# Attention decode with a fixed order of key and value tiles: two value tiles in one run of TensorE's loop, and whole landings for all keys but the last tile

## The chip, the cores and the metric

The kernel runs on one core of one Trainium2 chip. The metric is device time in microseconds (us) of one execution; a profile of one execution shows where it goes. "Span" is the time from the first to the last instruction of the program in that profile.

## The reference

One query per head attends to 65,536 keys. There are 32 query heads and 8 key/value heads (G = 8 in the kernel), so four query heads share one key/value head. All inputs and the output are bf16.

```python
B, Hq, Hkv, Sq, Sk, D = 1, 32, 8, 1, 65536, 128
scores = jnp.einsum("bhqd,bhkd->bhqk", q, k) * D ** -0.5
p = softmax(scores, axis=-1)
out = jnp.einsum("bhqk,bhkd->bhqd", p, v)
```

Keys and values together are 8 heads x 2 x 65,536 x 128 x 2 bytes = 268.4 MB, each byte read once.

## The kernel before, in words

**Tiles.** The keys of a head, and its values, are each cut into two tiles. A tile is 128 partitions x 256 rows (NT) x 128 elements, 64 KB in a partition and 8.4 MB in all. I write k0,1 for the second key tile of head 0 and v6,0 for the first value tile of head 6. There are 32 tiles and a ring of three buffers in SBUF (`buf`), so a tile can be asked for only when the tile three places earlier has been used up.

**Order of the tiles** (list `tiles`, L153 to L156): k0,0 k0,1 k1,0 k1,1 v0,0; then for each head g from 2 to 7 the four tiles kg,0 kg,1 v(g-2),1 v(g-1),0; then v6,1 v7,0 v7,1. All loads are issued by SyncE (SP) through `load` (L132), in that order, on one DMA queue. Before the load number `at`, SP waits for the use of tile `at - 3` (L161 to L169):

```python
if was == "k":
    sp.wait_ge(*((kb, wh + 1) if ws else (clr, 4 * wh + 3)))
else:
    if (wh, ws) not in BY:
        sp.wait_ge((sC, sD)[ws], 16 * (wh + 1)).then_inc(sV, NT // STEP)
    sp.wait_ge(vit, NT // STEP * (2 * wh + ws + 1))
```

`clr` is raised when TensorE clears one of its four score banks of a head; the third clear of a head (`4 * wh + 3`) tells that the head's first key tile has been read. `kb` is raised by VectorE once all four banks of the head are summed. `vit` is raised after each 32 value rows. A tile is loaded by one DMA or by several to consecutive rows; each DMA raises a semaphore of its own, so the first rows can be used before the last have landed. Before the change k0,0, k0,1, k7,0 and k7,1 come in two halves each, v6,0 and v6,1 in 128 + 128 rows, v7,0 in 128 + 64 + 64 (`BY`, L22 to L24), v7,1 in eight pieces (`PIECES`, L28).

**VectorE (DVE)** transposes each half of a key tile in place (`turn`, L312, the transpose at L318), waiting for that half's semaphore `sK[b][x]` (L315). Where a key tile lands by one DMA, the second half's semaphore has been raised beforehand by ScalarE (L254 to L258). After the four halves of a head comes the block `turned` (L365): it waits for the four score banks, copies a small value (L327, which raises `kb`), transposes half of the weights of the head before (L323), takes the maximum (L370), and exchanges a few small results with TensorE until the reciprocal at L337. Then it loops to the next head's keys.

**TensorE (PE)** runs a loop written out by blocks with its counters in registers. `turn` waits for the head's query weights (`wqs`); `bank` waits for one transposed half (`kt`), clears a score bank (L451, a matmul at L418) and runs 32 matmuls on it (L460), four banks a head. Then, from head 2 on, `values` (L479) runs v(g-2),1: each round takes one unit of `sV` and runs 8 matmuls on 32 value rows (L484). `summed` closes the sum of a head (L501), finds the common maximum (L504) and starts the next sum (L509, L511). Then `values` runs v(g-1),0 and control returns to `turn`. Register `x` tells `values_done` whether to go to `turn` (5) or on to `summed`; register `e` tells where a run of value rows ends. After the last keys `turn` goes to the block `late` (L518), which sets `e`, and from there to `values`. `tail` (L524) takes the last 64 rows of v7,1 as their pieces land.

**GpSimd (POOL)** passes the landings of the pieced value tiles on to `sV` (L215 to L220); after v6,0 it also waits for `outs` to reach 8 and raises `wqs` by 2, for the two late passes through `turn`. **ScalarE (ACT)** loads the queries (L227), takes the exponentials (L244) and writes the outputs.

Of the kernel before, what the change touches and what calls it, by code (L numbers as in the profile page):

```python
# [9 lines left out]
ALU = mybir.AluOpType  # L10
# [3 lines left out]
G = 8  # L14
# [3 lines left out]
NT = 256  # L18
# [1 line left out]
C = 16  # L20
SLIDE = P + 4 * (W - 1)
BY = {  # L22
    (G - 2, 0): (128, 128), (G - 2, 1): (128, 128), (G - 1, 0): (128, 64, 64),
}  # L24
N = 2
FAR = 2.0 ** 126
# [1 line left out]
PIECES = (64, 64, 32, 32, 44, 8, 8, 4)  # L28
MOVED = 4
# [3 lines left out]
def kernel(  # L33
# [18 lines left out]
    _, Hkv, Sk, _ = k.shape  # L52
# [5 lines left out]
    pe, dve, act, pool, sp = nc.tensor, nc.vector, nc.scalar, nc.gpsimd, nc.sync  # L58
# [37 lines left out]
    def sem(name):  # L96
        sems.append(nc.alloc_semaphore(name))
        return sems[-1]

    sK = [[sem(f"sK{b}{x}") for x in range(2)] for b in range(3)]  # L100
# [11 lines left out]
    wqs = sem("wqs")  # L112
# [7 lines left out]
    outs = sem("outs")  # L120
# [4 lines left out]
    cleared = list(sems)  # L125
# [3 lines left out]
    kr = [k[0, g].rearrange("(p n) d -> p (n d)", p=P) for g in range(G)]  # L129
    vr = [v[0, g].rearrange("(p n) d -> p (n d)", p=P) for g in range(G)]  # L130

    def load(at, src, s, lo=0, n=NT):  # L132
        at = at % 3 * half + lo * D
        return sp.dma_start(  # L134
            out=buf[:, at:at + n * D], in_=src[:, s * half + lo * D:s * half + (lo + n) * D]
        )

    first = load(0, kr[0], 0, 0, NT // 2)  # L140
    tc.no_tile_sem_insts.add(first.ins.name)
    first.then_inc(sK[0][0], 16)
    tc.add_to_no_dep_group("first", first.ins)
# [3 lines left out]
    tc.compile()  # L147


    load(0, kr[0], 0, NT // 2, NT // 2).then_inc(sK[0][1], 16)  # L150
    load(1, kr[0], 1, 0, NT // 2).then_inc(sK[1][0], 16)
    load(1, kr[0], 1, NT // 2, NT // 2).then_inc(sK[1][1], 16)
    tiles = [("k", 0, 0), ("k", 0, 1), ("k", 1, 0), ("k", 1, 1), ("v", 0, 0)]  # L153
    for g in range(2, G):
        tiles += [("k", g, 0), ("k", g, 1), ("v", g - 2, 1), ("v", g - 1, 0)]
# [2 lines left out]
    for at, (kind, h, s) in enumerate(tiles):  # L158
        if at < 2:
            continue  # L160
        if at > 2:  # L161
            was, wh, ws = tiles[at - 3]
# [4 lines that stand above are left out]
                if (wh, ws) not in BY:  # L167
                    sp.wait_ge((sC, sD)[ws], 16 * (wh + 1)).then_inc(sV, NT // STEP)
                sp.wait_ge(vit, NT // STEP * (2 * wh + ws + 1))  # L169
        if kind == "k" and h == G - 1:  # L170
            for x in range(2):
                load(at, kr[h], s, x * NT // 2, NT // 2).then_inc(sK[at % 3][x], 16)
        elif kind == "k":
            load(at, kr[h], s).then_inc(sK[at % 3][0], 16)
        elif (h, s) == (G - 1, 1):
            lo = 0
            for n, land in zip(PIECES, sP):
                load(at, vr[h], s, lo, n).then_inc(land, 16)
                lo += n
        elif (h, s) in BY:  # L180
            lo = 0
            for n in BY[h, s]:
                load(at, vr[h], s, lo, n).then_inc(lands.pop(0), 16)
                lo += n
        else:
            load(at, vr[h], s).then_inc((sC, sD)[s], 16)
# [29 lines left out]
    for at, (land, n) in enumerate(list(zip(sL, sum(BY.values(), ()))) + list(zip(sP, PIECES))[:MOVED]):  # L216

        pool.wait_ge(land, 32 if land is sP[0] else 16).then_inc(sV, n // STEP)
        if at + 1 == len(BY[G - 2, 0]):
            pool.wait_ge(outs, G).then_inc(wqs, 2)  # L220

    def take(engine, semaphore, n=1):

        engine.wait_ge(semaphore, n).then_inc(semaphore, -n)  # L224


    act.dma_start(out=qn, in_=q[0, :, 0, :]).then_inc(sQ, 16)  # L227
    act.wait_ge(qps, 1)
    act.copy(
        out=qx[:, :].rearrange("p (b r h) -> p b h r", b=2, r=2),  # L230
# [10 lines left out]
    for g in range(G + 1):  # L241
        if g < G:
            act.wait_ge(nms, g + 1)
            act.activation(  # L244
                out=E[:, :], in_=sc[:, :], func=ACT.Exp, bias=nmb[:, 0:1], scale=SCALE,
                accum_out=o_r[:, D:D + 1],
            ).then_inc(exd, 1)

        act.wait_ge(rls, g + 1)
        at = max(g - 1, 0) * D  # L250
        act.activation(  # L251
            out=o_out[:, at:at + D], in_=psum_f[0:H, 0:D], func=ACT.Copy, scale=rl
        ).then_inc(outs, 1)
        if g == 0:  # L254

            for b in range(3):
                n = sum(kind == "k" and at % 3 == b and 0 < h < G - 1 for at, (kind, h, _) in enumerate(tiles))
                act.nop().then_inc(sK[b][1], 16 * n)  # L258
    act.wait_ge(outs, G + 1)
    store(1, 0, G - 1)  # L260
    act.wait_ge(end, 1)
# [7 lines left out]
    def value(reg, below):  # L269
        return bass.RuntimeValue.of_register_unchecked(reg, min_val=0, max_val=below - 1)  # L270
# [68 lines left out]
    def block_of(engine):  # L339

        return lambda name: nc.body(name, parent=home, valid_engines=[engine.engine])

    block = block_of(dve)
    r_h, r_k = dve.alloc_register("h"), dve.alloc_register("k")
    h, kb_at = value(r_h, G + 1), value(r_k, 3)
# [61 lines left out]
    def counter(name, below):  # L407

        reg = pe.alloc_register(name)
        return reg, value(reg, below)  # L410

    block = block_of(pe)

    def add(reg, n, op=ALU.add):
        pe.reg_alu(reg, reg, n, op)

    def clear(bank, lhsT=zer[:, 0:P], rhs=zer):
        return pe.matmul(out=bank, lhsT=lhsT, rhs=rhs, start=True, stop=False)  # L418

    def close(bank):  # L420
        return pe.matmul(  # L421
            out=bank[:, 0:1], lhsT=zer[:, 0:P], rhs=zer[:, 0:1], start=False, stop=True
        )
# [5 lines left out]
    def chosen(out, start, n=D):  # L429

        return pe.matmul(out=out[0:H, 0:n], lhsT=sel[:, :], rhs=o_r[:, 0:n], start=start, stop=True)  # L431

    r_g, g = counter("g", G + 2)
    r_x, x = counter("x", 6)
    r_p, p = counter("p", ring)
    r_s, s = counter("s", 4 * W)
    r_w, w = counter("w", 2049)
    r_e, e = counter("e", 2049)
# [15 lines left out]
    with block("scores"):  # L454
        bank = sc[:, ds(value(r_x, 4) * 512, 512)]
        slide = value(r_s, 4 * (W - N) + 1)
        keys = value(r_p, ring - half // 2 + (W - N) * D + 1)
        for y in range(4 * N):
            m, n = y % 4, y // 4
# [40 lines left out]
    with block("summed"):  # L500
        close(psum_o[:, :]).then_inc(vdone, 1)  # L501
        take(pe, mxs)

        pe.matmul(  # L504
            out=misc[:, :], lhsT=same[:, :], rhs=each[:, :].unsqueeze(1).broadcast_to([P, 16, 32]),
            start=True, stop=True,
        ).then_inc(pes, 1)
        take(pe, mxs)
        clear(psum_o[:, :], away, rows4[:, :])  # L509
        pe.reg_mov(r_x, 5)  # L510
        chosen(psum_f, True, D + 1).then_inc(pes, 1)  # L511
        add(r_g, 1)
        pe.br_ne(g, 1, on_true="values", on_false="turn")
    with block("turn"):
        take(pe, wqs)
        pe.reg_mov(r_x, 0)
        pe.br_lt(g, G, on_true="bank", on_false="late")
    with block("late"):  # L518

        pe.reg_alu(r_e, r_g, 4 * (sum(PIECES[:MOVED]) - NT), ALU.mult)  # L520
        add(r_e, 2048 - 4 * G * (sum(PIECES[:MOVED]) - NT))
        pe.br("values")

    with block("tail"):  # L524
        at = sum(PIECES[:MOVED])
# [62 lines left out]
```

## Time and profile before

| What | us |
|---|---|
| Median of three runs (lowest, highest) | 628.53 (628.41, 628.55) |
| The profiled execution's own time | 628.39 |
| Its span | 626.5 |
| Time outside the span | 1.9 |
| PE busy / DVE busy within the span | 504.5 / 331.4 |

A row of a timeline has the start in us from the span's beginning, the length in us, the engine, the line, the operation, what is written and read, how many instructions were merged, and in brackets the idle time of the engine just before and what ended it. "PEq" and "DVEq" are the sequencers of the engines: their waits on semaphores end the idle time, whoever raised the semaphore. SPq rows are DMA issues, and all of them stand under L134. In a view by stages, PEclk is the TensorE clock that was granted, as a share of full speed.

### The profile page before, as it was taken

Reading aid. Unit: us, or ns where it says so; the run is one execution under the profiler, and the core shown is the slowest. Engines: PE = TensorE matmul, PEld = TensorE weight load, DVE = VectorE, ACT = ScalarE, POOL = GpSimd, SP = SyncE. Lnnn points to the kernel's source line nnn. Section 1 sums busy time; section 2 is a strip of 40 time slices with the busy share of each in tenths; the row PEclk is TensorE's granted clock in tenths of the full one; section 3 lists DMA queues with packets and bytes.
Section 4 is the critical chain, followed back from the end, with each engine's and each line's share of the span. In section 5 each row is a group of like instructions: output and inputs, shape, how many; then the busy total and the mean of one; then the engine's idle time right before and its main releaser. Section 6 shows DMA issues by size and latency. Waiting matters only on the chain. (4 is left out here: it accounts for less than half of the span.)

```text
span 626.5 us, 8015 instructions
## 1 busy us (share of the span) xinstructions
PE 504.5 (81%) x2186; PEld 204.2 (33%) x2186; DVE 331.4 (53%) x109; ACT 21.1 (3%) x28; POOL 6.0 (1%) x16
## 2 busy tenths in 40 slices
PE   0587299798994889948799397993979988799997
PEld 0232043243331333313333133331433333333333
DVE  3983895789214892148821588215872389410100
ACT  1000100100010000100001000010000100001000
POOL 2000000000000000000000000000000000000000
PEclk9998589799998789988899889997899998999999
DMA  9999999999999999999999999999999999999997
GB/s 371 433 469 402 469 402 469 402 460 410 452 418 423 448 402 469 402 469 402 469 402 469 402 469 402 469 402 469 402 464 406 418 425 429 435 435 435 423 431 319
DMA packets 6857, 268.46 MB, mean 429 GB/s; under 512 B 840, under 2 KB 968, under 8 KB 1224
## 3 DMA queue, kind: packets, MB, share of 16 engines
q1 hardware_dynamic: 6768, 268.44, 99.4%
q10 hardware_dynamic: 88, 0.02, 0.0%
q14 instruction: 1, 0.01, 0.0%
HBM read 268.44 MB, written 0.01 MB: 429 GB/s over the span
## 5 line engine op out<-in xcount | busy, mean ns | idle before, releaser
L318 DVE STREAM_TRANSPOSE buf<-buf 128x8192 f32<-128x8192 f32 x32 | 277.2, 8694 | 87.2 <-DVEq L224 87.2
L460 PE MATMUL sc<-buf,zeros 128*128 x1024 | 247.8, 401 | 0.0
L484 PE MATMUL psum_o<-buf,Ew 128*16 x1008 | 226.0, 382 | 11.7 <-PEq L224 11.0
L460 PEld LDWEIGHTS sc<-buf,zeros 128*128 x1024 | 102.3, 100 | 137.7 <-issue 41.6
L484 PEld LDWEIGHTS psum_o<-buf,Ew 128*16 x1008 | 89.3, 89 | 145.2 <-issue 54.9
L418 PE MATMUL sc<-zeros 128*128 128x512 bf16 x32 | 13.8, 432 | 87.8 <-PEq L224 87.8
L331 DVE TENSOR_REDUCE o_r<-psum_o 128x128 f32<-128x512 f32 x10 | 6.9, 688 | 100.2 <-DVEq L224 72.4
L327 DVE COPY o_r<-o_r 4x1 f32<-4x1 f32 x9 | 1.3, 142 | 79.7 <-DVEq L224 65.6
L418 PEld LDWEIGHTS sc<-zeros 128*128 128x128 bf16 x32 | 3.1, 98 | 97.1 <-issue 96.0
L244 ACT ACTIVATE zeros<-sc,nmb 128x2048 bf16<-128x2048 f32 x8 | 15.7, 1967 | 535.9 <-DVE nmb L382 535.9
L323 DVE STREAM_TRANSPOSE Ew<-zeros 128x1024 bf16<-128x1024 bf16 x18 | 22.3, 1240 | 14.0 <-PE psum_o L484 14.0
L504 PE MATMUL misc<-each,same 128*128 128x512 f32 x18 | 11.3, 712 | 8.6 <-PEq L224 8.6
L370 DVE TENSOR_REDUCE mx<-sc 128x1 f32<-128x2048 f32 x8 | 18.0, 2253 | 0.0
L441 PE MATMUL misc<-Ew 32*128 32x128 bf16 x1 | 0.3, 283 | 10.7 <-DVE Ew L308 10.7
L208 POOL TENSOR_TENSOR zeros<-qx,quad 128x64 bf16<-128x64 bf16 x8 | 2.4, 294 | 486.6 <-ACT o_out L251 480.4
L504 PEld LDWEIGHTS misc<-each,same 128*128 128x128 f32 x18 | 2.9, 202 | 8.9 <-issue 8.8
L421 PE MATMUL sc<-zeros 128*128 128x1 bf16 x32 | 5.2, 163 | 0.0
L418 PE MATMUL psum_o<-rows,zeros 4*128 4x512 bf16 x10 | 4.5, 451 | 0.0
L289 DVE CAST Ew<-ident 32x128 bf16<-32x128 f32 x1 | 3.0, 2984 | 2.7 <-POOL ident L193 2.7
L421 PEld LDWEIGHTS sc<-zeros 128*128 128x128 bf16 x32 | 3.0, 95 | 3.9
L251 ACT ACTIVATE o_out<-psum_f,o_r 4x128 bf16<-4x128 f32 x9 | 3.1, 345 | 29.3 <-DVE o_r L337 29.3
L431 PE MATMUL psum_f<-o_r,sel 128*4 128x129 f32 x18 | 3.9, 302 | 0.0
(32 smaller groups left out, 31.9 us busy)
## 6 DMA issues: line engine op xcount, KB each, us to landing
buf<-in_k_dram SPq DMA_DIRECT2D x8, 4096.0 KB, 28.5
buf<-in_v_dram SPq DMA_DIRECT2D x5, 4096.0 KB, 32.5
buf<-in_v_dram SPq DMA_DIRECT2D x4, 2048.0 KB, 36.4
buf<-in_v_dram SPq DMA_DIRECT2D x2, 1024.0 KB, 38.7
buf<-in_v_dram SPq DMA_DIRECT2D x1, 1408.0 KB, 42.6
buf<-in_v_dram SPq DMA_DIRECT2D x2, 256.0 KB, 40.6
buf<-in_k_dram SPq DMA_DIRECT2D x12, 34.6
buf<-in_v_dram SPq DMA_DIRECT2D x12, 34.4
```

What stands on the lines that cost most here:

```text
L244: act.activation(out=E[:, :], in_=sc[:, :], func=ACT.Exp, bias=nmb[:, 0:1], scale=SCALE, accum_out=o_r[:, D:D + 1],).then_inc(exd, 1)
L251: act.activation(out=o_out[:, at:at + D], in_=psum_f[0:H, 0:D], func=ACT.Copy, scale=rl).then_inc(outs, 1)
L318: dve.transpose(out=kv, in_=kv).then_inc(kt, 1)
L323: return dve.transpose(out=Ew[:, at], in_=E[:, at])
L331: return dve.tensor_reduce(out=o_r[:, 0:D], in_=psum_o[:, :].rearrange("p (y d) -> p d y", y=4), axis=AX.X, op=ALU.max)
L370: after(dve.tensor_reduce(out=mx[:, :], in_=sc[:, :], axis=AX.X, op=ALU.max))
L418: return pe.matmul(out=bank, lhsT=lhsT, rhs=rhs, start=True, stop=False)
L421: return pe.matmul(out=bank[:, 0:1], lhsT=zer[:, 0:P], rhs=zer[:, 0:1], start=False, stop=True)
L431: return pe.matmul(out=out[0:H, 0:n], lhsT=sel[:, :], rhs=o_r[:, 0:n], start=start, stop=True)
L460: pe.matmul(out=bank, lhsT=moved(wq[:, m * SLIDE + 4 * n:][:, 0:P], slide), rhs=moved(T[:, n, m // 2, m % 2], keys), start=False, stop=False,)
L484: last = pe.matmul(out=psum_o[0:16, :], lhsT=moved(Ew[:, column(4 * j + 3):][:, 0:16], weight), rhs=moved(buf[:, 4 * j * D:][:, 0:4 * D], ...
L504: pe.matmul(out=misc[:, :], lhsT=same[:, :], rhs=each[:, :].unsqueeze(1).broadcast_to([P, 16, 32]), start=True, stop=True,).then_inc(pes, 1)
```

## The change

1. k0,0, k0,1 and k7,0 land by one DMA each; only k7,1 is still cut in halves. ScalarE's raising of the second halves' semaphores covers them now, and stands ahead of its first wait instead of after head 0.
2. v6,0 lands by one DMA, v7,0 by two of 128 rows instead of three. v6,1 (two) and v7,1 (eight) are as they were.
3. TensorE sets `e` for the late runs in `summed`, between its first and second exchange with VectorE, and leaves `x` as it is there. So v6,0 and v6,1 are one run of `values`, and so are v7,0 and the first 192 rows of v7,1; neither passes through `values_done` and `turn` in its middle. The `wqs` signal for these passes is gone; GpSimd still holds v6,1 back until `outs` is 8. Heads below 8 pass through a new small block `first`, which sets `x` to 5 as `summed` did.

```diff
 BY = {
-    (G - 2, 0): (128, 128), (G - 2, 1): (128, 128), (G - 1, 0): (128, 64, 64),
+    (G - 2, 0): (NT,), (G - 2, 1): (128, 128), (G - 1, 0): (128, 128),
 }
...
-    first = load(0, kr[0], 0, 0, NT // 2)
+    first = load(0, kr[0], 0)
...
-    load(0, kr[0], 0, NT // 2, NT // 2).then_inc(sK[0][1], 16)
-    load(1, kr[0], 1, 0, NT // 2).then_inc(sK[1][0], 16)
-    load(1, kr[0], 1, NT // 2, NT // 2).then_inc(sK[1][1], 16)
+    load(1, kr[0], 1).then_inc(sK[1][0], 16)
...
-        if kind == "k" and h == G - 1:
+        if (kind, h, s) == ("k", G - 1, 1):
...
         if at + 1 == len(BY[G - 2, 0]):
-            pool.wait_ge(outs, G).then_inc(wqs, 2)
+            pool.wait_ge(outs, G)
...
     act.dma_start(out=qn, in_=q[0, :, 0, :]).then_inc(sQ, 16)
+
+    for b in range(3):
+        n = sum(kind == "k" and at % 3 == b and (h, s) != (G - 1, 1) for at, (kind, h, s) in enumerate(tiles))
+        act.nop().then_inc(sK[b][1], 16 * n)
     act.wait_ge(qps, 1)
...
-        if g == 0:
-
-            for b in range(3):
-                n = sum(kind == "k" and at % 3 == b and 0 < h < G - 1 for at, (kind, h, _) in enumerate(tiles))
-                act.nop().then_inc(sK[b][1], 16 * n)
...
         ).then_inc(pes, 1)
+        add(r_g, 1)
+        pe.br_lt(g, G, on_true="first", on_false="late")
+    with block("late"):
+
+        pe.reg_alu(r_e, r_g, 4 * (sum(PIECES[:MOVED]) - NT), ALU.mult)
+        add(r_e, 2048 - 4 * G * (sum(PIECES[:MOVED]) - NT))
+        pe.br("cleared")
+    with block("first"):
+        pe.reg_mov(r_x, 5)
+        pe.br("cleared")
+    with block("cleared"):
         take(pe, mxs)
         clear(psum_o[:, :], away, rows4[:, :])
-        pe.reg_mov(r_x, 5)
         chosen(psum_f, True, D + 1).then_inc(pes, 1)
-        add(r_g, 1)
         pe.br_ne(g, 1, on_true="values", on_false="turn")
     with block("turn"):
         take(pe, wqs)
         pe.reg_mov(r_x, 0)
-        pe.br_lt(g, G, on_true="bank", on_false="late")
-    with block("late"):
-
-        pe.reg_alu(r_e, r_g, 4 * (sum(PIECES[:MOVED]) - NT), ALU.mult)
-        add(r_e, 2048 - 4 * G * (sum(PIECES[:MOVED]) - NT))
-        pe.br("values")
+        pe.br("bank")
```

## The prediction

> **What bounds the kernel now.** I read the page's slices first, then the DMA queues, then the chain that ended last.
>
> ```profile
> span 626.5 us, 8015 instructions
> PE 504.5 (81%) x2186; PEld 204.2 (33%) x2186; DVE 331.4 (53%) x109; ACT 21.1 (3%) x28; POOL 6.0 (1%) x16
> ...
> DMA  9999999999999999999999999999999999999997
> ...
> q1 hardware_dynamic: 6768, 268.44, 99.4%
> ```
>
> The 16 DMA engines are at 9 in every slice but the last, and SP's queue (q1) holds them for 99.4% of the span. PE at 81% and DVE at 53% have air. So the kernel is one stream of 268.44 MB that starts once and never stops. Its time can change in three ways: the stream itself gets cheaper, it gets a hole, or what follows its end gets longer. The end of the chain confirms it:
>
> ```profile
> 563.41 14.21 PE psum_o L484 x64
> ...
> 579.43 42.63 DMA buf<-in_v_dram
> 622.06 0.04 issue
> 622.10 0.82 PE psum_o L533 x11
> ```
>
> A piece of v7,1 is asked for at 579.43, lands at 622.06, and only then does TensorE run its last matmuls. The 42.63 us are time in the queue behind other loads.
>
> Where could a hole come from? SP may ask for a tile only when the tile three places earlier is used up. At the start the user is VectorE, so its timeline and SP's belong side by side.
>
> ```profile
> 10.37 0.23 DVE L308 STREAM_TRANSPOSE Ew<-Ew 32x64 f32<-32x64 f32 x1 [4.36 <-DMA Ew<-in_q_dram]
> ...
> 13.04 8.71 DVE L318 STREAM_TRANSPOSE buf<-buf 128x8192 f32<-128x8192 f32 x1 [2.43 <-DVEq L224]
> 22.74 8.71 DVE L318 STREAM_TRANSPOSE buf<-buf 128x8192 f32<-128x8192 f32 x1 [0.99 <-DVEq L224]
> 32.45 8.71 DVE L318 STREAM_TRANSPOSE buf<-buf 128x8192 f32<-128x8192 f32 x1 [1.00 <-DVEq L224]
> 42.16 8.71 DVE L318 STREAM_TRANSPOSE buf<-buf 128x8192 f32<-128x8192 f32 x1 [1.00 <-DVEq L224]
> 60.45 0.14 DVE L327 COPY o_r<-o_r 4x1 f32<-4x1 f32 x1 [9.58 <-DVEq L224]
> ...
> 68.26 34.49 DVE L318 STREAM_TRANSPOSE buf<-buf 128x8192 f32<-128x8192 f32 x4 [0.64 <-DVEq L224]
> 110.69 0.14 DVE L327 COPY o_r<-o_r 4x1 f32<-4x1 f32 x1 [7.94 <-DVEq L224]
> ...
> 119.77 17.30 DVE L318 STREAM_TRANSPOSE buf<-buf 128x8192 f32<-128x8192 f32 x2 [1.43 <-DVEq L224]
> 139.13 17.30 DVE L318 STREAM_TRANSPOSE buf<-buf 128x8192 f32<-128x8192 f32 x2 [2.05 <-DVEq L224]
> ```
>
> ```profile
> 0.74 2.50 SPq L134 DMA_DIRECT2D buf<-in_k_dram  x4
> ...
> 94.87 0.33 SPq L134 DMA_DIRECT2D buf<-in_k_dram  x1
> ...
> 132.74 0.33 SPq L134 DMA_DIRECT2D buf<-in_v_dram  x1
> ```
>
> Head 0's four transposes start 9.70 us apart with 1 us of idle time between them: VectorE keeps pace with the halves as they land. Head 1's four run without a pause from 68.26; there VectorE is behind the stream. The rows at 119.77 and 139.13 start on the landings of k2,0 and k2,1, a whole tile apart: 19.36 us. So the load before k2,0 (v0,0) landed about 119.77 - 19.36 = 100.4, and SP asked for k2,0 at 94.87. That is only 5.5 us of cover, at the one place where VectorE is late already.
>
> **The change, part by part.**
>
> *Fewer DMAs.* Two halves take 9.70 + 9.71 = 19.41 us by those rows, a whole tile 19.36: a further DMA costs the full queue 0.05 us. Five go (k0,0, k0,1, k7,0, v6,0, v7,0), so the stream gains 0.25 us. The Trainium skill's page "DMA: Bandwidth & Descriptors" (section "Anatomy of one DMA") gives about 2.0 us fixed per DMA; by that, five would be 10 us. The spacing above speaks against adding it up in a full queue.
>
> *The first key tiles land whole.* Step by step, with times from VectorE's start on a landing:
>
> 1. The first transpose waits for all of k0,0: 22.74 - 0.05 = 22.7 instead of 13.04. Two in a row take 17.30, to 40.0. k0,1 is whole at 42.16 - 0.10 = 42.1, so its two end at 59.4. Before, the fourth ended at 42.16 + 8.71 = 50.9. Head 0's keys are transposed 8.5 us later: of the 9.7 us lost at the start only about 1.1 us come back, as the 1 us pauses close. ScalarE's moved semaphore raising and the queries' load (used at 10.37, the L308 row) lie beside this wait: even 12 us more of the load, which now shares the queue with larger pieces, would be covered until 22.7.
> 2. From the fourth transpose's end to the copy at L327 lies the last score bank. It took 9.58 us in head 0 and 7.94 in head 1, as TensorE's rows and clock show:
>
> ```profile
> 51.17 0.39 PE L418 MATMUL sc<-zeros 128*128 128x512 bf16 x1 [2.22 <-PEq L224]
> 51.55 8.74 PE L460 MATMUL sc<-buf,zeros 128*128 x32
> ...
> 103.05 0.39 PE L418 MATMUL sc<-zeros 128*128 128x512 bf16 x1 [1.08 <-PEq L224]
> 103.39 7.14 PE L460 MATMUL sc<-buf,zeros 128*128 x32
> ```
>
> ```profile
> 51.00:60.00 9.00, 8.83 (x33) 0.81 0.93 400
> 103.00:111.00 8.00, 7.67 (x35) 1.00 0.91 393
> ```
>
>    (stages: length, PE busy, PEclk, DMA share, GB/s). After 2.22 us of idle time the bank ran at a granted clock of 0.81, after 1.08 us at 1.00. In the changed kernel the last two transposes follow each other as in head 1, so I take 7.94 plus 0.2 for a possibly slow third bank: copy at 67.5. The other end is 9.58: 69.0.
> 3. From the copy to the next transpose: 68.26 - 60.45 = 7.81, so 75.3. Three transposes in a row take 34.49 - (34.49 - 17.30) / 2 = 25.9, to 101.2 (before: 94.16).
> 4. That third transpose of head 1 starts the third bank, whose clear lets SP ask for k2,0: 94.87 - 94.16 = 0.71 later, at 101.9. TensorE could be the later one there; its rows:
>
> ```profile
> 77.27 0.61 PE L418 MATMUL sc<-zeros 128*128 128x512 bf16 x1 [10.05 <-PEq L224]
> ...
> 94.45 0.39 PE L418 MATMUL sc<-zeros 128*128 128x512 bf16 x1 [0.24 <-PEq L224]
> ```
>
>    It begins the first bank at 77.27, right behind the first transpose (68.26 + 8.71 = 76.97), and idles 0.24 us before the third clear, so the two banks between are just hidden. They move by the same 7 us, and the 0.24 us stay.
> 5. At 101.9 the queue has been empty since about 100.3. An empty queue is seen once, at the start; the landing of the first DMA (issue at 0.74):
>
> ```profile
> DMA to landing us min/median/max: 12.2/12.2/12.2
> ```
>
>    It is used 0.1 us after that, at 13.04: 12.30 us from issue to use. The second half adds 19.36 - 9.70 = 9.66. k2,0 is then used at 101.9 + 21.96 = 123.9 instead of 119.77: **4.1 us later**. The start may include first-use costs. The other end is a restart at no cost: 101.9 + 19.36 + 0.1 = 121.4, **1.6 us later**. Less than that is excluded, as no byte moves before it is asked for. I take the start's price, the only row of an empty queue. The Trainium skill's page named above gives 2.0 us fixed, from a fit of DMAs issued by GpSimd; with it in place of the start's 12.30 - 9.70 = 2.6 the loss would be 3.5.
>
> Where does the delay go afterwards? All that is fed by the stream moves by 4.1, and VectorE and TensorE by 7.0, so they are 2.9 us later against the stream than before, until they next wait for a landing. The tightest load then is v0,1: 132.74 + 7.0 = 139.8, needed 2.6 us before k2,1 has landed, at 139.13 + 4.1 - 2.6 = 140.6. It holds by 0.8 us. Then VectorE waits for k2,1 again and the lag is gone.
>
> *k7,0 whole, and the late values.* At the end I use the times of before; the 4 us shift both sides.
>
> ```profile
> 497.17 8.71 DVE L318 STREAM_TRANSPOSE buf<-buf 128x8192 f32<-128x8192 f32 x1 [5.29 <-DVEq L224]
> 506.89 8.71 DVE L318 STREAM_TRANSPOSE buf<-buf 128x8192 f32<-128x8192 f32 x1 [1.01 <-DVEq L224]
> ...
> 545.86 15.66 PE L484 MATMUL psum_o<-buf,Ew 128*16 x64 [3.04 <-PEq L224]
> ...
> 578.65 14.21 PE L484 MATMUL psum_o<-buf,Ew 128*16 x64 [1.05 <-PEq L224]
> ...
> 594.94 14.05 PE L484 MATMUL psum_o<-buf,Ew 128*16 x64
> 610.01 3.71 PE L484 MATMUL psum_o<-buf,Ew 128*16 x16 [1.01 <-PEq L224]
> 614.02 7.14 PE L484 MATMUL psum_o<-buf,Ew 128*16 x32 [0.30 <-PEq L224]
> 622.10 0.82 PE L533 MATMUL psum_o<-buf,Ew 128*16 128x512 bf16 x11 [0.94 <-DMA buf<-in_v_dram]
> ```
>
> Head 7's transposes start at 506.8 and end 34.49 later, at 541.3; with 7.8 us for the last bank and about 1.1 to the values, v5,1 begins at 550.2 instead of 545.86, without the 3.04 us pause, so it takes 14.2 (the 578.65 row), to 564.4. The exchange before v6,0 took 563.41 - 561.52 = 1.9 us (545.86 + 15.66 = 561.52): 566.3. v6,0 and v6,1 are 28.4 us without the 1.05 us pause: 594.7 (before 592.86). The next exchange took 594.94 - 592.86 = 2.1: 596.8, then 112 matmuls at 7.14 / 32 = 0.22 us, 25 us: 621.8 at most (before 621.16). The piece of v7,1 they wait for lands at 622.06 - 0.25. So the two removed pauses just pay for k7,0's whole landing, and the tail waits for the stream as now. The new register steps stand where TensorE waits for VectorE (the second exchange), so they are hidden; without that cover they cost some 0.5 us twice (an estimate: half of the 1.05 us pause, whose passage held about twice as many steps).
>
> **The sum:** profiled 628.39 + 4.1 at k2,0 - 0.15 for the three later DMAs (the first two are in the 4.1) = **632.4 us**. The profiled execution is 0.14 below the median of 628.53; I leave that aside.
>
> **The rivals.**
>
> - *A second wait.* TensorE's clock falls longer in the sum of head 1, or at the end the new run comes after the last piece. A clock of 0.5 for 3.4 us more costs 1.7; against margins of 0.8 at v0,1 and near 0 at the end that adds 0.9 to 1.7: 633.3 to 634.1. For it: the margins are small. Against it: the pauses that lower the clock become shorter. 0.10.
> - *Not slower: the cover holds.* Decided at SP's request for k2,0. It has 5.5 us of cover, less 2.6 for the restart; a delay up to 2.9 us costs nothing and what is left is 0.25 us gained: 628.1. For it: everywhere later the loads are asked for earlier. Against it: the delay is worked out at 7.0 us, and between 22.7 and 101.9 VectorE has but one pause to lose, its wait for the score bank. 0.08.
> - *TensorE set the end.* Then two pauses of about 1.03 us go: 626.3. Against it: TensorE idles 0.94 us before L533, until a DMA. 0.03.
> - *A DMA's fixed price is paid even in a full queue.* At the empty queue's 2.6 us five fewer are 13 us: 615.4. The 9.70 us spacing leaves it 0.01. By the 2.0 us of the Trainium skill's page "DMA: Bandwidth & Descriptors" it would be 618.4.
>
> **How the numbers follow.** Forecast 0.78, with a range of its own from the ends above: 628.39 + 1.6 - 0.15 = 629.8 to 632.4 + 1.5 (bank of 9.58) = 633.9. The 8-in-10 range takes in most of the second wait: 629.8 to 634.2. This kernel's measurement tells about 0.2% (1.3 us) from no change: slower 0.86, same 0.10 (the cover, and the forecast's low edge), faster 0.04.
>
> **What would show it.** In the profile after: the first L318 at 22.7, head 0's copy near 67.5, SP's request for k2,0 near 101.9, and DMA below its usual rate in the slices around 100 to 103 us; the first L318 of head 2 near 123.9; the last landing 4 us later, with TensorE still idle before L533. I am wrong if k2,0 is asked for before 97.8, or if the stream shows a second hole.

## The result: one hole in the stream, 4.3 us lost

| | Median, us | Range, us | Runs |
|---|---|---|---|
| Before | 628.24 | 627.76 to 628.55 | 6 |
| After | 632.57 | 631.91 to 633.10 | 6 |

The ratio of after to before is 1.007, with a 95% interval of 1.006 to 1.0081. The forecast was 632.4. The profiled execution after the change took 632.96 (before: 628.39).

The page after the change, its span, slices and first queue:

```profile
span 631.1 us, 8000 instructions
...
DMA  9999996999999999999999999999999999999998
GB/s 399 415 449 428 436 461 270 461 403 461 403 399 465 415 449 453 411 461 403 465 399 465 399 465 399 465 399 465 399 465 399 465 399 465 411 453 413 428 424 331
...
q1 hardware_dynamic: 6048, 268.44, 98.7%
```

Each slice is 15.8 us. In the seventh, 94.7 to 110.4 us, the DMA engines are at 6 (busy for some six tenths of it) and move 270 GB/s, where every other slice but the last has 9 and 399 or more. (Rates of 399 and 465 in turn stand in the page before the change too, there as 402 and 469.) The queue's share fell from 99.4% to 98.7%. VectorE's timeline after the change shows what came late:

```profile
12.93 0.23 DVE L305 STREAM_TRANSPOSE Ew<-Ew 32x64 f32<-32x64 f32 x1 [6.93 <-DMA Ew<-in_q_dram]
22.73 17.30 DVE L315 STREAM_TRANSPOSE buf<-buf 128x8192 f32<-128x8192 f32 x2 [9.56 <-DVEq L222]
42.08 17.30 DVE L315 STREAM_TRANSPOSE buf<-buf 128x8192 f32<-128x8192 f32 x2 [2.04 <-DVEq L222]
67.35 0.14 DVE L324 COPY o_r<-o_r 4x1 f32<-4x1 f32 x1 [7.97 <-DVEq L222]
...
75.66 34.49 DVE L315 STREAM_TRANSPOSE buf<-buf 128x8192 f32<-128x8192 f32 x4 [0.64 <-DVEq L222]
118.09 0.14 DVE L324 COPY o_r<-o_r 4x1 f32<-4x1 f32 x1 [7.94 <-DVEq L222]
...
126.27 34.70 DVE L315 STREAM_TRANSPOSE buf<-buf 128x8192 f32<-128x8192 f32 x4 [0.64 <-DVEq L222]
```

The first transpose starts at 22.73, when k0,0 has landed whole. Head 1's four start at 75.66 instead of 68.26. The DMA issues of v0,0, k2,0 and v0,1 in SP's timeline, and how long the first two took to land:

```profile
67.52 0.33 SPq L134 DMA_DIRECT2D buf<-in_v_dram  x1
...
102.27 0.33 SPq L134 DMA_DIRECT2D buf<-in_k_dram  x1
...
139.41 0.33 SPq L134 DMA_DIRECT2D buf<-in_v_dram  x1
```

```profile
DMA to landing us min/median/max: 32.5/32.5/32.5
...
DMA to landing us min/median/max: 21.9/21.9/21.9
```

v0,0 landed at 67.5 + 32.5 = 100.0, and only 2.3 us later, at 102.27, was k2,0 asked for. It landed at 124.2. With a full queue it would have been 100.0 + 19.36 = 119.4: the hole is 4.8 us. Before, k2,0 was asked for at 94.87, ahead of the landing.

From the landings in the two traces the whole difference of the profiled executions, 4.57 us, can be laid out. k2,0 lands 4.54 later (124.18 against 119.64): the hole, less 0.3 us by which v0,0 was early. From k2,1 to k3,0 the loads come 0.64 us more late, as they follow each other a little slower (more on that at the end). From there to the 44-row piece (626.94 against 622.06) 0.30 comes back, of which three DMAs fewer explain 0.15. What follows that landing is 0.31 shorter (6.02 against 6.33), most of it in the storing of the output. 4.54 + 0.64 - 0.30 - 0.31 = 4.57.

### The profile page after: what moved, and what is told of

It reads as the page before. It is cut to its first block, busy times and chain, and to the rows that moved or that the text cites. A ratio compares the mean times of both kernels' runs of the same rounds, so it can differ in the third digit from the quotient of the medians.

```text
span 631.1 us, 8000 instructions
## 1 busy us (share of the span) xinstructions
PE 498.4 (79%) x2186; PEld 203.3 (32%) x2186; DVE 330.9 (52%) x109; ACT 21.1 (3%) x28; POOL 6.0 (1%) x16
## 3 DMA queue, kind: packets, MB, share of 16 engines
q1 hardware_dynamic: 6048, 268.44, 98.7%
## 5 line engine op out<-in xcount | busy, mean ns | idle before, releaser
L457 PE MATMUL sc<-buf,zeros 128*128 x1024 | 244.3, 397 | 0.0
L481 PE MATMUL psum_o<-buf,Ew 128*16 x1008 | 223.6, 379 | 6.6 <-PEq L222 6.6
L457 PEld LDWEIGHTS sc<-buf,zeros 128*128 x1024 | 101.8, 99 | 134.8 <-issue 37.1
## 6 DMA issues: line engine op xcount, KB each, us to landing
buf<-in_k_dram SPq DMA_DIRECT2D x15, 32.5
```

Source lines behind the costliest of these rows:

```text
L457: pe.matmul(out=bank, lhsT=moved(wq[:, m * SLIDE + 4 * n:][:, 0:P], slide), rhs=moved(T[:, n, m // 2, m % 2], keys), start=False, stop=False,)
L481: last = pe.matmul(out=psum_o[0:16, :], lhsT=moved(Ew[:, column(4 * j + 3):][:, 0:16], weight), rhs=moved(buf[:, 4 * j * D:][:, 0:4 * D], ...
```

## The experiments

The theory is that of the prediction: VectorE's late finish of head 0's keys delays the request for k2,0 beyond its cover, and the stream has a hole. Three rivals stood against it: the late values or k7,0 make the loss; what is lost is VectorE's late start as such; or whole landings cost something themselves.

### Half of the change at a time

**The first two tiles in halves again**, the rest of the change kept.

```diff
-    first = load(0, kr[0], 0)
+    first = load(0, kr[0], 0, 0, NT // 2)
...
-    load(1, kr[0], 1).then_inc(sK[1][0], 16)
+    load(0, kr[0], 0, NT // 2, NT // 2).then_inc(sK[0][1], 16)
+    load(1, kr[0], 1, 0, NT // 2).then_inc(sK[1][0], 16)
+    load(1, kr[0], 1, NT // 2, NT // 2).then_inc(sK[1][1], 16)
```

(ScalarE raises the semaphores for the other whole tiles after head 0, as before.)

> The changed kernel with k0,0 and k0,1 in halves again; k7,0 whole and the late values in one run are kept. Theory (the loss is one hole in the stream before k2,0, made by the first two tiles landing whole): the hole of 4.8 us is gone, k2,0 is asked for near 94.9 us again, and three DMAs fewer than before are left: 628.1 us, 0.15 under the kernel before. Rival (the late values or k7,0 make the loss): 630 us or more, and k2,0 asked for near 94.9 all the same.

Measured: 627.87 us, ratio 0.9998 (0.9989 to 1.0008). k2,0 was asked for at 94.41. The loss is gone; the gain of 0.15 us that was forecast is smaller than the interval and can't be told from none.

**Only the first two tiles whole**, on the kernel before.

```diff
-    first = load(0, kr[0], 0, 0, NT // 2)
+    first = load(0, kr[0], 0)
...
-    load(0, kr[0], 0, NT // 2, NT // 2).then_inc(sK[0][1], 16)
-    load(1, kr[0], 1, 0, NT // 2).then_inc(sK[1][0], 16)
-    load(1, kr[0], 1, NT // 2, NT // 2).then_inc(sK[1][1], 16)
+    load(1, kr[0], 1).then_inc(sK[1][0], 16)
```

(ScalarE's raising stands ahead of its first wait, as in the changed kernel.)

> The kernel before with only k0,0 and k0,1 landing whole. Theory: the whole hole, k2,0 asked for near 102.2 us, and 0.15 more than the changed kernel for the three DMAs kept: 632.7 us. Rival (late values or k7,0): 628.2 us.

Measured: 632.70 us, ratio 1.0077 (1.0062 to 1.0092), k2,0 asked for at 102.51. So these two landings make the whole loss, and the late values and k7,0 together none that can be measured.

### Which of the two tiles it is

**k0,0 in halves, k0,1 whole.** The rest is as in the changed kernel, but for ScalarE: in this kernel and the next it raises ahead of its first wait only the one semaphore that the whole one of the two tiles needs, and the others after head 0, as before the change.

```diff
-    first = load(0, kr[0], 0)
+    first = load(0, kr[0], 0, 0, NT // 2)
...
+    load(0, kr[0], 0, NT // 2, NT // 2).then_inc(sK[0][1], 16)
     load(1, kr[0], 1).then_inc(sK[1][0], 16)
```

> The changed kernel with k0,0 in halves, k0,1 still whole. Theory (what counts is the end of head 0's fourth transpose, not the start of the first): VectorE starts at 13.0 us but waits for the whole of k0,1 at 42.1, so the fourth transpose ends at 59.4 as in the changed kernel and k2,0 is asked for at 102.2: 632.5 us, nothing won. Rival (the late start is what is lost): about 628.1 us.

**k0,0 whole, k0,1 in halves.**

```diff
-    load(1, kr[0], 1).then_inc(sK[1][0], 16)
+    load(1, kr[0], 1, 0, NT // 2).then_inc(sK[1][0], 16)
+    load(1, kr[0], 1, NT // 2, NT // 2).then_inc(sK[1][1], 16)
```

> The changed kernel with k0,0 whole and k0,1 in halves. Theory: VectorE starts at 22.7 us and then runs four transposes without a pause, 34.5 us, to 57.2 instead of 59.4; the request for k2,0 comes 2.2 us earlier than in the changed kernel and the hole is 4.8 - 2.2 = 2.6 us: 630.4 us. Rival (the late start is what is lost): 632.5 us, nothing won.

Measured: 632.46 us for k0,0 in halves, ratio 1.0073 (1.0058 to 1.0088), and 630.23 us for k0,1 in halves, ratio 1.0034 (1.002 to 1.0047). VectorE's rows, first with k0,0 in halves:

```profile
13.02 8.71 DVE L319 STREAM_TRANSPOSE buf<-buf 128x8192 f32<-128x8192 f32 x1 [3.53 <-DVEq L223]
22.71 8.71 DVE L319 STREAM_TRANSPOSE buf<-buf 128x8192 f32<-128x8192 f32 x1 [0.98 <-DVEq L223]
42.06 17.30 DVE L319 STREAM_TRANSPOSE buf<-buf 128x8192 f32<-128x8192 f32 x2 [10.64 <-DVEq L223]
68.02 0.14 DVE L328 COPY o_r<-o_r 4x1 f32<-4x1 f32 x1 [8.65 <-DVEq L223]
```

then with k0,1 in halves:

```profile
22.68 34.49 DVE L319 STREAM_TRANSPOSE buf<-buf 128x8192 f32<-128x8192 f32 x4 [9.57 <-DVEq L223]
65.15 0.14 DVE L328 COPY o_r<-o_r 4x1 f32<-4x1 f32 x1 [7.98 <-DVEq L223]
```

The start at 13.02 wins nothing: what was won is lost in 10.64 us of waiting for the whole of k0,1, and the copy comes at 68.02. The start at 22.68 costs less, since no pause follows it: the copy is at 65.15, and k2,0 is asked for at 100.07 instead of 102.37. So it is the end of the four transposes that counts, not their start. The rival of the late start, which expected the two times the other way round, falls. Nor does the place of ScalarE's raising make the loss: with k0,0 in halves it is back behind head 0 but for one step, and the whole loss is there.

### Making VectorE late without touching a landing

To tell a cost of whole landings from VectorE's lateness, I made VectorE late in the kernel before, by idle reductions whose result nobody reads. **The first place was a poor one**: between head 0's transposes and its score exchange, one reduction or three.

```diff
+    with block("hold"):
+        for _ in range(3):
+            after(dve.tensor_reduce(
+                out=junk[:, :], in_=ident[:, :].unsqueeze(1).broadcast_to([P, 16, P]), axis=AX.X, op=ALU.max
+            ))
+        dve.br("turned")
```

> The kernel before, all tiles in their old pieces, with one idle reduction on VectorE between head 0's transposes and its score exchange. I estimate it at 2.3 us from the 2.25 us of the maximum over as many elements. Theory (5.5 us of cover before k2,0, of which a restart of the empty queue takes 2.55, so 2.9 are free): 2.3 us cost nothing, 628.2 us, while the request for k2,0 moves from 94.9 to 97.2. Rival 1 (each us that VectorE is late at the start is lost): 630.5. Rival 2 (the loss is a cost of whole landings, not of VectorE's lateness): 628.2.

> The same with three such reductions in head 0, 6.9 us by the same estimate. Theory: 6.9 - 2.9 = 4.0 us of hole before k2,0, 632.2 us, with the request for k2,0 near 101.8. Rival 1: 635.1. Rival 2 (a cost of whole landings): 628.2, as no landing is changed.

Measured: 627.83 us with one, ratio 0.9997 (0.9987 to 1.0006), and 628.59 with three, ratio 1.0009 (0.9999 to 1.0019). The second expectation missed by 3.6 us, and VectorE's rows with three show why:

```profile
50.84 7.11 DVE L367 TENSOR_REDUCE junk<-ident 128x16 f32<-128x2048 f32 x3
58.89 0.14 DVE L328 COPY o_r<-o_r 4x1 f32<-4x1 f32 x1 [0.94 <-DVEq L225]
```

The 7.11 us lie in a stretch in which VectorE would have waited for TensorE's last score bank in any case; 0.94 us of that wait are left. VectorE was busier, but not later: k2,0 was asked for at 93.82, where 101.8 was expected, and with one reduction at 93.66, where 97.2 was expected. These two runs say nothing on the theory.

**The second place is on the path**: behind head 0's reciprocal, ahead of head 1's first transpose.

```diff
-        dve.br_lt(h, G, on_true="keys", on_false="last")
+        dve.br_eq(h, 1, on_true="pause", on_false="again")
+    with block("pause"):
+        for _ in range(3):
+            after(dve.tensor_reduce(
+                out=junk[:, :], in_=ident[:, :].unsqueeze(1).broadcast_to([P, 16, P]), axis=AX.X, op=ALU.max
+            ))
+        dve.br("keys")
+    with block("again"):
+        dve.br_lt(h, G, on_true="keys", on_false="last")
```

> The kernel before, all tiles in their old pieces, with one idle reduction on VectorE after head 0's reciprocal, ahead of head 1's first transpose, where TensorE has nothing left to do beside it. Three took 7.1 us in the kernel hold3, so one is 2.3 us, with the branch 2.5. Theory: k2,0 was asked for 5.4 to 6.3 us before v0,0's landing in the kernels with the old pieces, 2.55 of it go to the restart, so 2.9 to 3.7 us of lateness are free: no loss, 628.0 us. Rival 1 (each us that VectorE is late there is lost): 630.5. Rival 2 (a cost of whole landings): 628.0.

> The same with three reductions, 7.1 us and with the branch 7.4. Theory: 7.4 less 2.9 to 3.7 is a hole of 3.7 to 4.5 us before k2,0: 631.7 to 632.5 us, with no landing changed, and k2,0 asked for near 101.5. Rival 1: 635.4. Rival 2: 628.0.

Measured: 628.10 us with one, ratio 1.0005 (0.9996 to 1.0015), and 631.95 with three, ratio 1.0059 (1.0042 to 1.0075). SP's request for k2,0 with one and then with three:

```profile
96.21 0.33 SPq L135 DMA_DIRECT2D buf<-in_k_dram  x1
```

```profile
101.11 0.33 SPq L135 DMA_DIRECT2D buf<-in_k_dram  x1
```

v0,0 landed at 100.0 in both. At 3.8 us ahead of that landing the request came in time: k2,0 landed 19.36 us after v0,0, and the median is that of before. (Two of the ten executions took 629.35 and 629.98 us; they have no trace, and why stays open.) At 1.1 us behind it, k2,0 landed 3.5 us late, with every tile in its old pieces. That is the kink which only the theory forecast: one pause free, three dear. Neither a loss in proportion to the lateness nor a cost of whole landings gives it.

The five kernels with a hole agree on its price. The hole is what k2,0's landing lies behind v0,0's, less 19.36:

| Kernel | v0,0 landed | k2,0 asked for | k2,0 landed | Hole | Hole less lateness |
|---|---|---|---|---|---|
| After | 99.98 | 102.27 | 124.18 | 4.84 | 2.55 |
| Only the first two whole | 99.99 | 102.51 | 124.29 | 4.94 | 2.42 |
| k0,0 in halves | 100.25 | 102.37 | 124.27 | 4.66 | 2.54 |
| k0,1 in halves | 100.00 | 100.07 | 122.12 | 2.76 | 2.69 |
| Three pauses | 100.04 | 101.11 | 122.94 | 3.54 | 2.47 |

The lateness is the request's time less v0,0's landing. An empty queue costs 2.4 to 2.7 us beyond it in all five, whether the first tiles land whole or in halves, and their median times lie above that of before by the hole within 0.6 us. The other side of the kink is seen most closely in the kernel with k0,1 in halves: there v0,1 was asked for at 138.62, 2.85 us before k2,1 landed, and landed 19.35 us after it, without a loss.

### What k7,0 costs at the end

**Only k7,0 whole**, on the kernel before, with the pauses between the late values kept.

```diff
-        if kind == "k" and h == G - 1:
+        if (kind, h, s) == ("k", G - 1, 1):
```

(and ScalarE raises the second half's semaphore for k7,0.)

> The kernel before with only k7,0 landing whole. Theory (at the end two changes cancel: k7,0's whole landing makes TensorE's values late by about 2 us, and the two pauses of 1.05 us that the new run removes pay for it): with the pauses kept TensorE reaches the 44-row piece about 2.1 - 0.17 = 1.9 us after its landing, 630.1 us, and no idle time before L533. Rival (TensorE has room enough at the end in any case): 628.2 us, with idle time before L533.

Measured: 630.18 us, ratio 1.0035 (1.0022 to 1.0047). TensorE's rows at the end:

```profile
550.30 14.23 PE L484 MATMUL psum_o<-buf,Ew 128*16 x64 [1.50 <-PEq L224]
...
581.73 14.21 PE L484 MATMUL psum_o<-buf,Ew 128*16 x64 [1.05 <-PEq L224]
...
613.09 10.71 PE L484 MATMUL psum_o<-buf,Ew 128*16 x48 [1.01 <-PEq L224]
623.96 0.82 PE L533 MATMUL psum_o<-buf,Ew 128*16 128x512 bf16 x11 [0.16 <-issue]
```

The piece landed at 621.64, but TensorE reached it at 623.96, 2.3 us later (1.9 were expected), with no pause on a DMA. In the changed kernel the two pauses of 1.05 and 1.01 us are gone and it just arrives in time:

```profile
571.77 28.21 PE L481 MATMUL psum_o<-buf,Ew 128*16 x128
...
602.10 24.71 PE L481 MATMUL psum_o<-buf,Ew 128*16 x112
626.98 0.82 PE L534 MATMUL psum_o<-buf,Ew 128*16 128x512 bf16 x11 [0.17 <-DMA buf<-in_v_dram]
```

So two parts of the change cancel: k7,0 in one landing alone costs 2.1 us (630.18 against 628.08), as it makes TensorE late, and the longer run pays that back. With both and the first two tiles in halves the time was 627.87 against 627.88, so together they gained nothing that was measured.

## Why the prediction was right, point by point

- **What bounds the kernel** held: the stream. Time was lost only where the stream stopped (first two tiles) or where TensorE fell behind its end (k7,0 alone).
- **Fewer DMAs, 0.05 us each**: k1,0, the tile behind the two whole ones, landed at 61.28 instead of 61.38. In the total time it can't be seen. The rival of a fixed price per DMA in a full queue fell: with three fewer the time was 627.87 against 627.88 us, not 8 us less. The Trainium skill's 2.0 us per DMA ("DMA: Bandwidth & Descriptors", section "Anatomy of one DMA") is near what the restart of an empty queue cost here, 2.4 to 2.7 us, and was not paid in a full one.
- **Steps 1 and 2**: the fourth transpose ended at 42.08 + 17.30 = 59.4 (forecast 59.4), the copy came at 67.35 (67.5). The choice of 7.94 over 9.58 for the last bank was right; the wait was 7.97. The reason given for it, the length of the pause ahead of a bank, is not enough: in the changed kernel the third bank came after the same 2.22 us of idle time that went before the slow bank of the prediction, and ran at a granted clock of 1.00 in 7.14 us, not at 0.81 in 8.74:

```profile
51.09 0.39 PE L415 MATMUL sc<-zeros 128*128 128x512 bf16 x1 [2.22 <-PEq L222]
51.43 7.14 PE L457 MATMUL sc<-buf,zeros 128*128 x32
```

  So the 0.2 us for a slow third bank were not spent here. They were with only the first two tiles whole: its third bank took 8.80 us at 0.81, and the wait was 8.21. The queries were used at 12.93 instead of 10.37, and that was covered, as forecast. (Their load does not share SP's queue, as I wrote: it is issued by ScalarE, and the profile has it on q10, beside q1 with the keys and values.)
- **Step 3** was 0.5 us short. From the copy to head 1's first transpose it took 75.66 - 67.35 = 8.31, not 7.81. TensorE's f32 matmuls in that exchange, first in the kernel before, then after:

```profile
64.61 1.54 PE L504 MATMUL misc<-each,same 128*128 128x512 f32 x2 [4.28 <-PEq L224]
```

```profile
71.51 2.05 PE L501 MATMUL misc<-each,same 128*128 128x512 f32 x2 [4.00 <-PEq L222]
```

  They took 2.05 us instead of 1.54. That is the whole 0.5, and the granted clock goes with it. Before, it was 1.00 up to 65.12, in the middle of these matmuls, and 0.50 from there on; after, it was 0.50 over all of them. Where it was 1.00 throughout (before, at 561.49) two such matmuls took 1.10 us. The term was read from a place where the clock changed, and carried over as if it were fixed.
- **Step 4**: the request at 102.27 (forecast 101.9; step 3 adds 0.5 to that, and step 2 takes off 0.15). TensorE did not become the later one: it idled 0.90 us before the third clear.

```profile
101.85 0.39 PE L415 MATMUL sc<-zeros 128*128 128x512 bf16 x1 [0.90 <-PEq L222]
```

- **Step 5**: the start's price of an empty queue, 2.6 us, was the right one of the two ends: 2.55 measured. Nothing points to first-use costs in it: counted to the landing, the start cost 12.90 - 0.74 - 9.70 = 2.46, no more than the later restarts.
- **Afterwards**: no second hole, as forecast. v0,1 was asked for at 139.41 (139.8), 4.1 us before k2,1 landed. One sign was stated wrongly: I wrote that head 2's first transpose would start near 123.9. k2,0 was there at 124.2, but VectorE was itself still 2 us behind and started at 126.27. I had worked out that lag (2.9 us) and not applied it to this sign; it costs no time.
- **The end**: TensorE idles 0.17 us before its last 11 matmuls, against 0.94 before. The forecast of "near 0" margin held. The last landing came 4.9 us later than before (628.60 against 623.72), not 4.

The mechanism and its place were right; that the sum came within 0.2 us of the median is partly luck. It was built on profiled executions, and there it is 0.6 short (632.96): k2,0 came 4.54 later, not 4.1, the slower loads behind it cost 0.64 that the sum does not have, and 0.46 more than it counts on came back on the way to the end and behind the 44-row piece. The median happens to lie 0.4 below the profiled execution.

## What to carry to other kernels

A stream that fills its queue all the time still has a place with the least cover: find, for each load, how long before the previous landing it is asked for, and subtract the restart of an empty queue (here 2.4 to 2.7 us). In these runs a request that came 2.85 us or more ahead of the landing opened no hole, and each us behind the landing was lost in full, with the restart on top; what counted was the end of the engine's chain, not its start. Joining the two halves of a tile saved 0.05 us in the full queue, and cost the head start that the first piece gave.

## What the runs showed that I had not expected

In some executions a few loads follow each other slower than the usual 19.36 us, without a gap. Before, k1,1 came 19.55 after k1,0; after, v0,1 came 19.69 after k2,1; with k0,0 in halves, k1,0 came 19.56 after k0,1. The place differs from kernel to kernel, and the kernel with only the first two tiles whole, equal to the changed one there, showed 19.35 for v0,1. A short cover is not what it takes: v0,1 had 4.1 us of cover after the change, and 3.2 with only the first two tiles whole. It adds up to 0.6 us in an execution. What causes it stays open.
